# A decode layer on one core: w1 behind the last V, the MLP at the end, and 240 rows of w2 on five DMA engines

## The chip, the cores and the metric

The kernel runs on one core of one Trainium2 chip. The metric is the device time of one execution in microseconds (us), as the median of several runs. One further execution was taken by the hardware profiler; all spans and durations come from it.

## What is computed

One layer for two sequences with one new token each (B = 2, D = 576). The token is normalized, and two branches work on it side by side: attention over the last 4,096 positions of a cache, and a two-layer MLP with a squared ReLU. Everything is bfloat16.

```python
xn = layernorm(x)                                # (2, 576)
q = xn @ wq                                      # 32 heads of 128
k, v = k_cache[:, :, -4096:], v_cache[:, :, -4096:]   # 16 kv heads, 2 q heads each
o = softmax(q k^T * 128**-0.5) v
h = relu(xn @ w1 + b1) ** 2                      # F = 4608
out = x + o @ wo + h @ w2 + b2
```

The weights and the cached keys and values are read once, some 53.6 MB in all; the arithmetic on them is small.

## The kernel before

**Attention in units.** There are 8 units `u` (4 groups of 4 kv heads, times 2 sequences). A unit has one K tile and one V tile of 2 MB (128 partitions of 16 KB). `step(u)` transposes K on TensorE in 8 groups of 8 (`transposes`, L230), copies each group out of PSUM on ScalarE or VectorE (L233, L235), computes scores (L245) and starts the softmax of the unit (L251 to L268), which runs on VectorE, GpSimd and ScalarE. `pv` (L282) multiplies with V two units later. After both sequences of a group, `wo_sel` (a product called `wps`, L301, and a cast `ws`, L304) and `wo_acc` (L209) add the group's part of `o @ wo` to `out_ps`.

**The MLP.** `mlp_h_block(c)` (L322) multiplies the c-th block of 128 rows of `w1` (four blocks, and a folded remainder) with `xn`, one matmul for each 128 of the 4,608 hidden columns: 36 chunks `CH`, each reading its weights with a step of `FR` = 18 columns, so that hidden index `p*18 + r` lies on partition `p`. After the last block VectorE adds b1 and squares (L326, L330) into `hT_sb`. `mlp_o` multiplies each chunk of `hT_sb` with 128 rows of w2, in two halves of 288 columns that go to different partitions of `out_ps` (`out_acc`, L209): two matmuls for a chunk.

**Order and queues.** Nearly all loads are issued on SP's queue in the order written, and each waits on SP until its buffer is free. K, V and the pieces of w2 share a pool `kv` of 6 buffers; wq and w1 share `wbig` of 4. Before, the order is: wq mixed with K of unit 0, K1, w1 blocks 0 and 1, V0, K2, the rest of w1, V1, wo(0), K3; then with each step V(u), wo and K(u+2); at the end the six pieces of w2 (`W2P`, 9 rows a partition down to 1). The h-blocks run inside steps 1 and 2; the outputs of w2 run as its pieces land, mixed with the last unit's `pv` and `wo_acc`. A framework inserts the waits and may shift instructions within an engine's list.

Of the kernel before, what the change touches and what calls it, by code (L numbers as in the profile page):

```python
# [9 lines left out]
BF16 = mybir.dt.bfloat16  # L10
# [6 lines left out]
def kernel(  # L17
# [14 lines left out]
    nc = tc.nc  # L32
    P = 128
    B, Sq, D = A_x.shape
    _, Hkv, Sk, Dh = A_k_cache.shape
    Hq = A_wq.shape[1] // Dh
    F = B_w1.shape[1]
# [11 lines left out]
    NU = NQ * B  # L49
# [9 lines left out]
    LQ = (Hq * Dh) // S  # L59
    L1 = F // S  # L60
    FR = L1 // P
    CH = [(s * L1 + r, FR, P) for s in range(S) for r in range(FR)]
    NFC = len(CH)
    OH = D // 2
    WR = NC * Dh // P
# [44 lines left out]
    def issue_w1(c):  # L110
        issue_w(w1_tiles, B_w1, c, "w1", F, L1)
# [9 lines left out]
    def issue_wo(tq):  # L121
        tl = wopool.tile([P, WR, D], BF16, tag="wo_sb", name=f"wo_{tq}")
        n = NC * Dh
        nc.sync.dma_start(out=tl[:], in_=A_wo[tq * n:(tq + 1) * n, :].rearrange("(p r) n -> p r n", r=WR))
        wo_tiles[tq] = tl

    def issue_w2(s, r0, r1):
        tl = kvpool.tile([P, (r1 - r0) * D], BF16, tag="kv", name=f"w2_{s}_{r0}")
        rows = B_w2[s * L1:(s + 1) * L1, :].rearrange("(p r) n -> p (r n)", r=FR)
        nc.sync.dma_start(out=tl[:], in_=rows[:, r0 * D:r1 * D])  # L130
        w2_tiles[(s, r0)] = tl

    x_sb = const.tile([B, D], BF16, name="x_sb")
    nc.scalar.dma_start(out=x_sb[:], in_=x2d)
# [113 lines left out]
    def softmax(u):  # L248
        sc_ps = sc_tiles.pop(u)
        m1 = work.tile([P, NC], F32, tag="m1", name=f"m1_{u}")  # L250
        nc.vector.tensor_reduce(out=m1[:], in_=sc_ps[:].rearrange("p j c -> p c j"), axis=AX.X, op=ALU.max)  # L251
        m2 = work.tile([P, NC], F32, tag="m2", name=f"m2_{u}")
        nc.vector.tensor_tensor(out=m2[:], in0=m1[:], in1=offm_f, op=ALU.subtract)  # L253
        gmax = work.tile([P, NC], F32, tag="gmax", name=f"gmax_{u}")
        nc.gpsimd.partition_all_reduce(gmax[:], m2[:], channels=P, reduce_op=ReduceOp.max)  # L255
        gm2 = work.tile([P, NC], F32, tag="gm2", name=f"gm2_{u}")
        nc.vector.tensor_tensor(out=gm2[:], in0=gmax[:], in1=offm_f, op=ALU.add)
        sub = work.tile([P, NJ, NC], F32, tag="sub", name=f"sub_{u}")
        nc.vector.tensor_tensor(out=sub[:], in0=sc_ps[:], in1=gm2[:].unsqueeze(1).to_broadcast([P, NJ, NC]),  # L259
                                op=ALU.subtract)  # L260
        pT = keep.tile([P, NJ, NC], BF16, tag="pT", name=f"pT_{u}")
        nc.scalar.activation(out=pT[:], in_=sub[:], func=ACT.Exp, scale=scale)  # L262
        l1 = work.tile([P, NC], F32, tag="l1", name=f"l1_{u}")
        nc.vector.tensor_reduce(out=l1[:], in_=pT[:].rearrange("p j c -> p c j"), axis=AX.X, op=ALU.add)  # L264
        lsum = work.tile([P, NC], F32, tag="lsum", name=f"lsum_{u}")
        nc.gpsimd.partition_all_reduce(lsum[:], l1[:], channels=P, reduce_op=ReduceOp.add)  # L266
        rinv = keep.tile([P, NC], F32, tag="rinv", name=f"rinv_{u}")
        nc.vector.reciprocal(out=rinv[:], in_=lsum[:])  # L268
        pT_tiles[u] = pT
        rinv_tiles[u] = rinv  # L270
# [3 lines left out]
    def pv(u, g):  # L274
        tq, b = divmod(u, B)
        if g == 0:
            oT_cur[u] = psum.tile([P, NC], F32, tag="misc", bufs=2, name=f"oT_ps_{u}")
        oT_ps = oT_cur[u]
        v_sb = v_tiles[u]
        for i in range(JG):  # L280
            j = g * JG + i
            nc.tensor.matmul(oT_ps[:], lhsT=v_sb[:, j * Dh:(j + 1) * Dh], rhs=pT_tiles[u][:, j, :],  # L282
                             start=(j == 0), stop=(j == NJ - 1))
        if g == NG - 1:
            if b == 0:
                oG_tiles[tq] = keep.tile([P, NC, B], BF16, tag="oG", name=f"oG_{tq}")
            nc.vector.tensor_tensor(out=oG_tiles[tq][:, :, b], in0=oT_ps[:], in1=rinv_tiles.pop(u)[:], op=ALU.mult)
            pT_tiles.pop(u)
# [3 lines left out]
    def wo_sel(tq):  # L292
        oG = oG_tiles.pop(tq)
        rr = work.tile([P, WR, NC * B], BF16, tag="rr", name=f"rr_{tq}")
        nc.vector.tensor_tensor(
            out=rr[:],
            in0=oG[:].rearrange("p h b -> p (h b)").unsqueeze(1).to_broadcast([P, WR, NC * B]),
            in1=rmask[:].unsqueeze(2).to_broadcast([P, WR, NC * B]), op=ALU.mult)
        wps = psum.tile([P, WR, B], F32, tag="misc", bufs=2, name=f"wps_{tq}")
        for h in range(NC):  # L300
            nc.tensor.matmul(wps[:], lhsT=sel[:, h, :, :].rearrange("p a c -> p (a c)"),  # L301
                             rhs=rr[:, :, h * B:(h + 1) * B], start=(h == 0), stop=(h == NC - 1))
        ws = work.tile([P, WR, B], BF16, tag="ws", name=f"ws_{tq}")
        nc.vector.tensor_copy(out=ws[:], in_=wps[:])  # L304
        wo_state[tq] = ws
# [9 lines left out]
    def mlp_h_block(c):  # L315
        if c == 0:
            mlp["ps"] = psum.tile([P, NFC, B], F32, tag="misc", bufs=2, name="hT_ps")
            nc.vector.memset(mlp["ps"][:], 0.0)
        hT_ps = mlp["ps"]
        for i, (f0, step, m) in enumerate(CH):  # L320
            lhsT, xc = w_operands(w1_tiles, c, f0, L1, step, m)
            nc.tensor.matmul(hT_ps[0:m, i, :], lhsT=lhsT, rhs=xnT[:, xc, :],  # L322
                             start=(c == 0 and i == 0), stop=(c == KC - 1), skip_group_check=True)
        if c == KC - 1:
            t1 = work.tile([P, NFC, B], F32, tag="t1", name="t1")
            nc.vector.tensor_tensor(out=t1[:], in0=hT_ps[:],  # L326
                                    in1=b1_sb[:].unsqueeze(2).to_broadcast([P, NFC, B]),
                                    op=ALU.add)
            hT_sb = const.tile([P, NFC, B], BF16, name="hT_sb")
            nc.vector.scalar_tensor_tensor(out=hT_sb[:], in0=t1[:], scalar=0.0, in1=t1[:],  # L330
                                           op0=ALU.max, op1=ALU.mult)
            mlp["h"] = hT_sb

    def mlp_o(s, r0, r1, last=False):
        w2_sb = w2_tiles.pop((s, r0))
        for r in range(r0, r1):
            o = (r - r0) * D
            out_acc(mlp["h"][:, s * FR + r, :], lambda a, z: w2_sb[:, o + a:o + z], stop=(last and r == r1 - 1))

    def load_k(u):  # L340
        for f in issue_kv(k_tiles, A_k_cache, u, "k"):
            f()

    def load_v(u):
        for f in issue_kv(v_tiles, A_v_cache, u, "v"):
            f()

    W2P = [(0, 0, 9), (0, 9, 18), (1, 0, 9), (1, 9, 14), (1, 14, 17), (1, 17, 18)]

    load_k(1)  # L350
    issue_w1(0)
    issue_w1(1)
    load_v(0)
    load_k(2)
    for c in range(2, KC):
        issue_w1(c)
    load_v(1)
    issue_wo(0)
    load_k(3)
    def step(u, hooks):  # L360
        for g in range(NG + 2):
            if g < NG:
                transposes(u, g)
            if u >= 2 and 1 <= g <= NG:
                pv(u - 2, g - 1)
            if g >= 2:
                scores(u, g - 2)
            for f in hooks.get(g, ()):
                f()
        softmax(u)  # L370

    def load_next(u):
        load_v(u)
        if u % B == 0:
            issue_wo(u // B)
        if u + 2 < NU:
            load_k(u + 2)

    for g in range(4):
        transposes(0, g)  # L380
    q_block(0)
# [5 lines left out]
    for g in range(NG):  # L387
        scores(0, g)
    softmax(0)
    b1_sb = const.tile([P, NFC], BF16, name="b1_sb")  # L390
    nc.gpsimd.dma_start(out=b1_sb[:].rearrange("p (s r) -> p s r", s=S), in_=B_b1.rearrange("(s p r) -> p s r", s=S, p=P))  # L391
    b2_sb = const.tile([1, D], BF16, name="b2_sb")
    nc.gpsimd.dma_start(out=b2_sb[:], in_=B_b2.rearrange("(o n) -> o n", o=1))
    step(1, {})
    mlp_h_block(0)
    mlp_h_block(1)
    out_acc(ident[:B, :B], lambda a, z: x_sb[:, a:z], start=True)
    out_acc(ones_b[:, :], lambda a, z: b2_sb[:, a:z])
    for u in range(2, NU):
        hooks = {}  # L400
        if u >= 4 and u % B == 0:
            hooks = {3: [lambda t=u // B - 2: wo_sel(t)], 6: [lambda t=u // B - 2: wo_acc(t)]}
        step(u, hooks)
        if u == 2:
            for c in range(2, KC):
                mlp_h_block(c)
        load_next(u)
    for w in W2P:
        issue_w2(*w)
    for g in range(NG):  # L410
        pv(NU - 2, g)
    wo_sel(NQ - 2)
    wo_acc(NQ - 2)
    for g in range(NG):
        pv(NU - 1, g)
    mlp_o(*W2P[0])
    wo_sel(NQ - 1)
    mlp_o(*W2P[1])
    wo_acc(NQ - 1)
    for i in range(2, len(W2P)):  # L420
        mlp_o(*W2P[i], last=(i == len(W2P) - 1))

    fin_sb = work.tile([32 + B, OH], BF16, tag="fin", name="fin_sb")
# [33 lines left out]
```

## Time and profile before

| | |
|---|---|
| median of 3 runs | 137.17 us (137.09 to 137.22) |
| the profiled execution, whole / span | 137.33 / 135.4 us |
| mean granted TensorE clock | 0.761 of full |
| busy: TensorE / VectorE / ScalarE / GpSimd | 76 / 40 / 32 / 7% |
| loaded from HBM | 53.62 MB, 396 GB/s over the span |
| TensorE instructions (matmuls and weight loads) | 2,054 + 2,054 |

How to read the views. The page cuts the span in 40 slices; a digit is a busy share in tenths, PEclk the TensorE clock granted, DMA the mean share of the 16 DMA engines. A line of a group names source line, engine (PE for matmuls, PEld for weight loads), output and inputs, the count, the busy time, and the mean of one in ns; behind the last bar stands the idle time just before them and what ended it. A timeline line gives start, length and count. The chain of waits follows back from the last instruction what released each step. TensorE's ends are modelled, so rates are taken from start to start.

### The profile page before, as it was taken

The page shows a single profiled execution, that of the slowest core. Times are in us where ns is not written, and L with a number is a line of the kernel's source. Part 1 is how long each engine was busy: PE and PEld are TensorE (multiplying, and loading weights), DVE is VectorE, ACT ScalarE, POOL GpSimd, SP SyncE. Part 2 cuts the span into 40 slices and gives each one's busy share as a digit, 9 for nine tenths or more (in the row PEclk, how much of TensorE's full clock was granted, in tenths as well). Part 3 has the DMA queues.
Part 4 walks back from the last instruction along what each step waited for, and adds up shares of the span by engine and source line. Part 5 has one row for each costly group of instructions (what it writes and reads, how often), then busy time and mean ns, then how long its engine had stood idle before and what let it go on. Part 6 is the DMA issues. An engine that isn't in the chain of part 4 may idle for free.

```text
span 135.4 us, 4461 instructions
## 1 busy us (share of the span) xinstructions
PE 102.7 (76%) x2054; PEld 93.3 (69%) x2054; DVE 53.7 (40%) x125; ACT 42.8 (32%) x47; POOL 9.9 (7%) x31
## 2 busy tenths in 40 slices
PE   0049937599978999609992994999599839977791
PEld 0039937589968999609983994899499739554450
DVE  7512411574252433502464345625544564541001
ACT  6704630155013711004601550741155065100000
POOL 7300000110110001100011001100100110110000
PEclk9999995559955995555896589658658999655589
DMA  3999999999999999999999999999999999999940
GB/s 126 401 427 426 426 438 409 415 439 436 411 420 408 439 421 426 415 431 411 436 431 426 421 431 416 406 450 411 436 421 423 425 411 437 416 406 423 393 177 1
DMA packets 5422, 53.90 MB, mean 398 GB/s; under 512 B 646, under 2 KB 796, under 8 KB 1308
## 3 DMA queue, kind: packets, MB, share of 16 engines
q1 hardware_dynamic: 5332, 53.61, 94.4%
q8 instruction: 16, 0.26, 0.8%
q10 hardware_dynamic: 8, 0.00, 0.1%
q0 software_dynamic: 64, 0.01, 0.1%
q14 instruction: 2, 0.02, 0.0%
HBM read 53.62 MB, written 0.00 MB: 396 GB/s over the span
## 4 chain that ended last, share of the span: by engine, by line
DMA 69%; PE 23%; DVE 3%; POOL 2%; issue 1%; ACT 0%; SPq 0%; POOLq 0%
DMA k<-in_A_k_cache_dram 41%; DMA w<-in_B_w_dram 24%; PE kT_ps L230 13%; DMA b_sb<-in_B_b_dram 4%; PE sc_ps L245 3%; PE oT_ps L282 3%; PE out_ps L209 2%; PE qT_ps L218 1%; DVE l L264 1%; POOL b_sb L391 1%; POOL sel L197 1%; DVE sub L259 1%; ACT pT L262 0%; DVE kT L235 0%; DVE fin_sb L424 0%
## 5 line engine op out<-in xcount | busy, mean ns | idle before, releaser
L230 PE MATMUL kT_ps<-ident,k 128*128 128x128 bf16 x512 | 49.7, 267 | 13.9 <-DMA k<-in_A_k_cache_dram 13.6
L230 PEld LDWEIGHTS <-k 128*128 128x128 bf16 x512 | 41.0, 122 | 14.6 <-DMA k<-in_A_k_cache_dram 14.3
L233 ACT COPY kT<-kT_ps 128x1024 bf16<-128x1024 bf16 x32 | 32.2, 1011 | 38.6 <-PE kT_ps L230 38.3
L235 DVE COPY kT<-kT_ps 128x1024 bf16<-128x1024 bf16 x32 | 21.9, 687 | 33.0 <-PE kT_ps L230 33.0
L245 PE MATMUL sc_ps<-qT_all,kT 128*128 128x8 bf16 x512 | 22.1, 168 | 2.8 <-ACT kT L233 1.4
L245 PEld LDWEIGHTS <-kT 128*128 128x128 bf16 x512 | 20.0, 102 | 4.2 <-ACT kT L233 1.8
L282 PE MATMUL oT_ps<-pT,v 128*128 128x8 bf16 x512 | 16.3, 167 | 0.4 <-DMA v<-in_A_v_cache_dram 0.4
L262 ACT ACTIVATE pT<-sub 128x512 bf16<-128x512 f32 x8 | 5.0, 630 | 35.9 <-DVE sub L259 35.9
L282 PEld LDWEIGHTS <-v 128*128 128x128 bf16 x512 | 14.8, 99 | 1.5 <-DMA v<-in_A_v_cache_dram 1.0
L264 DVE TENSOR_REDUCE l<-pT 128x8 f32<-128x512 bf16 x8 | 8.5, 1059 | 4.7 <-ACT pT L262 4.7
L322 PE MATMUL hT_ps<-xnT,w 128*128 128x2 bf16 x144 | 9.8, 201 | 0.0
L322 PEld LDWEIGHTS <-w 128*128 128x128 bf16 x144 | 9.4, 161 | 0.0
L251 DVE TENSOR_REDUCE m<-sc_ps 128x8 f32<-128x512 f32 x8 | 5.5, 692 | 9.1 <-PE sc_ps L245 8.8
L255 POOL PARTITION_ALL_REDUCE gmax<-m x8 | 2.9, 365 | 83.9 <-DVE m L253 77.6
L209 PE MATMUL out_ps<-w,hT_sb 128*2 128x288 bf16 x72 | 7.2, 363 | 1.3 <-DMA w<-in_B_w_dram 1.3
L209 PE MATMUL out_ps<-wo,ws 128*2 128x288 bf16 x64 | 6.8, 359 | 0.3 <-DVE ws L304 0.3
L209 PEld LDWEIGHTS <-hT_sb 128*2 128x2 bf16 x72 | 3.9, 102 | 4.2 <-issue 1.8
L259 DVE TENSOR_TENSOR sub<-sc_ps,gm 128x512 f32<-128x512 f32 x8 | 5.5, 692 | 0.3
L218 PE MATMUL qT_ps<-xnT,wq 128*128 128x2 bf16 x128 | 3.9, 164 | 2.3 <-DMA wq<-in_A_wq_dram 2.0
L218 PEld LDWEIGHTS <-wq 128*128 128x128 bf16 x128 | 3.8, 99 | 2.4 <-DMA wq<-in_A_wq_dram 2.1
L209 PEld LDWEIGHTS <-ws 128*2 128x2 bf16 x64 | 3.1, 99 | 2.8 <-issue 0.6
L266 POOL PARTITION_ALL_REDUCE lsum<-l x8 | 3.2, 398 | 24.5 <-DVE l L264 24.5
(59 smaller groups left out, 35.1 us busy)
## 6 DMA issues: line engine op xcount, KB each, us to landing
v<-in_A_v_cache_dram SPq DMA_DIRECT2D x8, 2048.0 KB, 29.4
k<-in_A_k_cache_dram SPq DMA_DIRECT2D x7, 2048.0 KB, 26.3
w<-in_B_w_dram SPq DMA_DIRECT2D x4, 1152.0 KB, 18.1
wo<-in_A_wo_dram SPq DMA_DIRECT2D x4, 1152.0 KB, 27.5
wq<-in_A_wq_dram SPq DMA_DIRECT2D x4, 1024.0 KB, 9.0
w<-in_B_w_dram SPq DMA_DIRECT2D x3, 1296.0 KB, 22.3
k<-in_A_k_cache_dram SPq DMA_DIRECT2D x2, 1024.0 KB, 8.8
w<-in_B_w_dram SPq DMA_DIRECT2D x1, 720.0 KB, 16.7
```

The lines of the kernel that those rows point to most:

```text
L209: nc.tensor.matmul(out_ps[32 * i:32 * i + B, :], lhsT=lhsT, rhs=rhs_of(i * OH, (i + 1) * OH), start=start, stop=stop, skip_group_check=True)
L218: nc.tensor.matmul(qT_ps[:, h, :], lhsT=lhsT, rhs=xnT[:, xc, :], start=(c == 0 and h == 0), stop=(c == KC - 1), skip_group_check=True)
L230: nc.tensor.transpose(out=kT_ps[:, i * P:(i + 1) * P], in_=k_sb[:, j * Dh:(j + 1) * Dh], identity=ident[:])
L233: nc.scalar.copy(out=kT[:], in_=kT_ps[:])
L235: nc.vector.tensor_copy(out=kT[:], in_=kT_ps[:])
L245: nc.tensor.matmul(sc_ps[:, g * JG + i, :], lhsT=kT[:, i * P:(i + 1) * P], rhs=qT_all[:, b, tq * NC:(tq + 1) * NC], start=True, stop=True)
L251: nc.vector.tensor_reduce(out=m1[:], in_=sc_ps[:].rearrange("p j c -> p c j"), axis=AX.X, op=ALU.max)
L259: nc.vector.tensor_tensor(out=sub[:], in0=sc_ps[:], in1=gm2[:].unsqueeze(1).to_broadcast([P, NJ, NC]), op=ALU.subtract)
L262: nc.scalar.activation(out=pT[:], in_=sub[:], func=ACT.Exp, scale=scale)
L264: nc.vector.tensor_reduce(out=l1[:], in_=pT[:].rearrange("p j c -> p c j"), axis=AX.X, op=ALU.add)
L282: nc.tensor.matmul(oT_ps[:], lhsT=v_sb[:, j * Dh:(j + 1) * Dh], rhs=pT_tiles[u][:, j, :], start=(j == 0), stop=(j == NJ - 1))
L322: nc.tensor.matmul(hT_ps[0:m, i, :], lhsT=lhsT, rhs=xnT[:, xc, :], start=(c == 0 and i == 0), stop=(c == KC - 1), skip_group_check=True)
```

## The change

1. All of w1 is issued later: blocks 0 and 1 right behind V7, then wo(3), the rest of w1, and w2. V and K move up by one unit instead, and wo(1), wo(2), wo(3) get places of their own.
2. The h-blocks move from steps 1 and 2 to the end, around the last `wo_acc`; all outputs of w2 follow them.
3. The second half of w2's rows is cut anew. 16 rows a partition on 128 partitions (`FT`), then 240 rows (`XR` = 12 on each of `XP` = 20 partitions), then 16 rows (`XQ`). The 240 rows load in four transfers whose leading dimension is `XE` = 5, spread among the K and V loads; the 16 rows follow as `w2y_sb`.
4. The chunks change with it: 18 with step 18, 16 with step 16, 12 of 20 hidden columns with step 12, and one of 16; 47 in place of 36. `mlp_x` does the outputs of the last 13 ahead of the others.
5. b1 loads in four pieces behind a memset, and b2 now goes out ahead of them.

```diff
+    XR, XP, XE = 12, 20, 5
+    FT = (L1 - XR * XP) // P
+    CH = [(r, FR, P) for r in range(FR)] + [(L1 + r, FT, P) for r in range(FT)]
+    CH += [(FX0 + r, XR, XP) for r in range(XR)] + [(FX0 + XR * XP, 1, XQ)]
...
+    def issue_w2x():
+        if x_parts:
+            i = x_parts.pop(0)
+            rows = B_w2[FX0:FX0 + XR * XP, :].rearrange("(e i r) n -> i e (r n)", e=XE, r=XR)
+            nc.sync.dma_start(out=w2x_sb[i:XP:XP // XE, :], in_=rows[i])
+            if not x_parts:
+                nc.sync.dma_start(out=w2y_sb[:], in_=B_w2[FX0 + XR * XP:F, :])
...
+    def mlp_x():
+        for i, (f0, step, m) in enumerate(CH[FR + FT:]):
+            w = w2x_sb[0:m, i * D:(i + 1) * D] if m == XP else w2y_sb[:]
+            out_acc(mlp["h"][0:m, FR + FT + i, :], lambda a, z: w[:, a:z])
...
-    W2P = [(0, 0, 9), (0, 9, 18), (1, 0, 9), (1, 9, 14), (1, 14, 17), (1, 17, 18)]
+    W2P = [(0, 0, 9), (0, 9, 18), (1, 0, 9), (1, 9, 13), (1, 13, 15), (1, 15, 16)]
...
     load_k(1)
-    issue_w1(0)
-    issue_w1(1)
     load_v(0)
     load_k(2)
-    for c in range(2, KC):
-        issue_w1(c)
     load_v(1)
...
-    mlp_h_block(0)
-    mlp_h_block(1)
+    load_k(4)
+    issue_wo(1)
...
+        if u + 1 < NU - 1:
+            load_v(u + 1)
+        if u + 3 < NU:
+            load_k(u + 3)
+        if u == 4:
+            issue_wo(2)
+        if u == 5:
+            load_v(NU - 1)
+            issue_w1(0)
+            issue_w1(1)
+        if u == 6:
+            issue_wo(3)
             for c in range(2, KC):
-                mlp_h_block(c)
-        load_next(u)
-    for w in W2P:
+                issue_w1(c)
+            for w in W2P[:2]:
+                issue_w2(*w)
+    for w in W2P[2:4]:
         issue_w2(*w)
     for g in range(NG):
         pv(NU - 2, g)
+    issue_w2(*W2P[4])
     wo_sel(NQ - 2)
     wo_acc(NQ - 2)
     for g in range(NG):
         pv(NU - 1, g)
-    mlp_o(*W2P[0])
+    issue_w2(*W2P[5])
+    mlp_h_block(0)
+    mlp_h_block(1)
     wo_sel(NQ - 1)
-    mlp_o(*W2P[1])
     wo_acc(NQ - 1)
-    for i in range(2, len(W2P)):
+    for c in range(2, KC):
+        mlp_h_block(c)
+    mlp_x()
+    for i in range(len(W2P)):
         mlp_o(*W2P[i], last=(i == len(W2P) - 1))
```

## The prediction

> **What bounds the kernel now.** I read the page's slices first, then the chain of waits, then windows over the last microseconds, then the timeline of TensorE and the groups by line.
>
> ```profile
> PE   0049937599978999609992994999599839977791
> PEclk9999995559955995555896589658658999655589
> DMA  3999999999999999999999999999999999999940
> q1 hardware_dynamic: 5332, 53.61, 94.4%
> q8 instruction: 16, 0.26, 0.8%
> ```
>
> The DMA row is 9 from the second slice to the last but two: the transfers bound this kernel, 53.62 MB in 132 us. TensorE is only partly busy, and its granted clock swings between half and full. The chain of waits ends on the transfers:
>
> ```profile
> 116.33 15.67 DMA w<-in_B_w_dram
> 132.00 0.04 issue
> 132.04 0.67 PE out_ps L209 x8
> 132.72 0.03 issue
> 132.74 0.45 DVE fin_sb L424
> ```
>
> The last pieces of w2 land at 132.0, eight matmuls follow, then the copy and the store: 2.7 us from the last matmul's end (132.7) to the span's end. But the transfers do not end together (columns: window, length, PE, PEld, DVE, ACT, POOL busy, clock, DMA share, GB/s):
>
> ```profile
> 127.00:128.00 1.00, 1.00 (x12) 0.57 (x10) 0.00 (x0) 0.00 (x0) 0.00 (x0) 0.50 1.05 423
> 128.00:129.00 1.00, 1.00 (x12) 0.55 (x10) 0.00 (x0) 0.00 (x0) 0.00 (x0) 0.50 0.80 310
> 129.00:130.00 1.00, 1.00 (x12) 0.53 (x8) 0.00 (x0) 0.00 (x0) 0.00 (x0) 0.52 0.67 255
> 130.00:131.00 1.00, 1.00 (x22) 0.71 (x18) 0.00 (x0) 0.00 (x0) 0.00 (x0) 1.00 0.42 165
> 131.00:131.90 0.90, 0.89 (x16) 0.51 (x11) 0.00 (x0) 0.00 (x0) 0.00 (x0) 1.00 0.30 106
> ```
>
> From 128 on the DMA share sinks: about six of the sixteen engines are done near 129, seven work on until 132. So the end is set by late engines, and a perfect levelling would give 0.2+0.33+0.58+0.63 = 1.7 us.
>
> [...]
>
> **The change, part by part.** *Transfers.* The bytes are the same. 240 of w2's rows (0.276 MB) leave the even share: eleven engines carry 17.3 KB less, 0.65 us at 26.6 GB/s per engine (425 over 16); the five carry 38 KB more, 1.43 us. If the five are among the early engines, the last landing moves from 132.4 to 131.7; if among the late, to 133.8. The profile does not name engines; I take the former, and keep -0.65 and +1.4. The loads that wait for buffers stay far ahead: in the new SP order k5 waits for step 2's transposes (near 42 us) and is due at 71; w2's last piece waits for pv(7) (near 109) and is due at 131. Five more issues on SP cost 0.3 to 0.5 us each beside that lead: nothing. On POOL a memset and three more small b1 loads (some 1 us each, as L391) delay `sel` (busy from 4.75 now) to about 6; first need is after 55 us: nothing. b2 is now issued ahead of b1 and lands up to 1 us sooner, which TensorE only turns into a longer wait for wq (2.05 us idle at 19.5): nothing.
>
> *The middle.* Five h-blocks leave steps 1 and 2: 5 x 2.24 us. TensorE has idle time there, so no gain, and it waits longer for k.
>
> *The end.* This is the price. Counting bytes back from 131.7 at 0.418 MB/us (k1 landing at 25.7, k2 at 41.1, k3 at 60.9 fit that line), k7 lands at 91.5, v7 at 104.3, w1 pieces at 107, 109.9, 115.6, 118.4, 119.8, with wo(3) at 112.7, and w2 from 123 to 131.7. TensorE's built order after the scores of unit 7 is pv(6), wps(2), wo(2), pv(7), wps(3), h(0), h(1), wo(3), h(2), h(3), h(rem), then 26 matmuls on the five-engine rows and 68 on the rest.
>
> ```profile
> 50.13 2.37 PE L322 MATMUL hT_ps<-xnT,w 128*128 128x2 bf16 x36
> 52.37 2.37 PE L322 MATMUL hT_ps<-xnT,w_rem 128*128 128x2 bf16 x36
> 119.73 1.87 PE L282 MATMUL oT_ps<-pT,v 128*128 128x8 bf16 x64 [0.44 <-DMA v<-in_A_v_cache_dram]
> 126.02 2.32 PE L209 MATMUL out_ps<-w,hT_sb 128*2 128x288 bf16 x18 [0.82 <-DMA w<-in_B_w_dram]
> 128.13 2.04 PE L209 MATMUL out_ps<-wo,ws 128*2 128x288 bf16 x16
> 130.01 1.88 PE L209 MATMUL out_ps<-w,hT_sb 128*2 128x288 bf16 x28
> L218 PEld LDWEIGHTS <-wq 128*128 128x128 bf16 x128 | 3.8, 99 | 2.4 <-DMA wq<-in_A_wq_dram 2.1
> ```
>
> An h-block of 36 takes 2.24 us start to start, 62 ns each, at either clock. The q-block on contiguous weights takes 32 in 0.99 us, 31 each. h reads w1's columns with a step of 18, so the weight load sets its pace. [...] One block: 2.1 + 0.4 = 2.5 us. An output pair costs 0.235 us at half clock (16 matmuls in 1.88 us from 128.13), about 0.12 at full (14 pairs in 1.6).
>
> Step 7 starts at 91.5 and takes 7.5 to 8.7 without pv (24 transposes in 2.74 us at half clock; before, 8.8 with 1.1 of pv inside). Scores end near 99.6. The cast of ws(2) stands behind softmax(7) in VectorE's order: 5.0 us from the row maximum to the reciprocal (115.71 to 120.6), 0.4 more. wo(2) waits for it on TensorE and pv(7) is queued behind: 105.1. Then wo(2) 2.0, pv(7) 1.8, its scaling, spreading and wps(3) 0.95: 109.9. h(0), h(1): 114.9. wo(3) 2.0: 116.9. h(2), h(3), h(rem) at 2.5, all after their landings: 124.4. Two VectorE operations of 0.23 each at 72 columns, 0.25 at 94, with handovers 0.75: hT is ready at 125.1. [...] Last matmul: 125.1 + 8.2 + 0.3 latency = 133.6, against 132.7. Sum: +0.9; I take 0.2 off, because step 7 runs at full clock in a third of such cases or so (7.5 instead of the 8.1 used): +0.7. The profiled execution took 137.33 us, span 135.4 plus 1.9 around it; the median of three is 137.17. From the median: **137.9 us, slower**.
>
> **Rivals.** *The output work hides (not slower).* Place: TensorE from 116 on. If hT is ready by 123.5, 1.6 us earlier than worked out, the last output matmuls wait for the last landing again, and the levelling comes through whole: -0.65, 136.5 us. It needs h-blocks of 2.0 us or less (full-column loads under 50 ns), or the full clock at the start of the outputs (47 x 0.12 = 5.6 us, in time even from 125.7). For it: the DMA-bound tail is short, 0.67 us. Against it: 144 loads at a median of 162 ns with the step of 18, 96 without. It decides from 124.2 for break-even.
> *Short loads are not short.* All 47 at 62 ns make 2.9 us a block; three blocks behind landed data and two before add 2.1: +2.8, 140.0 us. For it: no row of the profile shows a strided load of few columns.
> *The five engines are the late ones.* Last landing 133.8, then 0.7: +1.4, 138.6 us. For it: about ten of sixteen engines still work past 129, and the profile does not say which. [...] One in five.
> *The change not made as said*: the built SP order has all w1 pieces behind v7, and 5-row transfers among the k and v loads; dismissed.
>
> **How the numbers follow.** Forecast 0.45 (own range 137.2 to 138.8), hidden 0.18, all loads long 0.17, late five 0.20. Measurement tells about 0.2%, 0.27 us, from no change. Faster takes nearly all of the first rival and the very lowest end of the forecast: 0.18. Within 0.2%: 0.12, the forecast's low end. Slower: 0.70. The range runs from 136.5 to 140.3, which takes in both bounds of the levelling and the long loads, and leaves out a step of 16 at 75 ns with a late clock, and h at 31 ns with a clock already full.
>
> **What would show it.** Right: no DMA wait above 0.5 us before the last output group; PEclk 0.50 when the outputs start near 125; DMA share falling to 0 about 1.5 us before the last matmul; the chain ending in out_ps and hT_ps matmuls instead of w2. The levelling is right if the sinking of the DMA share after 128 becomes a steeper one ending 0.65 us sooner. Wrong: the last output group still ended by a DMA wait, blocks of 47 far from 2.5 us, or a share near 0.3 (five engines) in the last microseconds.

## The result, and the profile after

The changed kernel takes 142.88 us (median of 4 runs, 141.15 to 144.69) against 137.19 us: a ratio of 1.033, 95% interval 1.0258 to 1.0402. Run again unchanged beside the first experiments it took 143.74 us (143.15 to 145.03), ratio 1.0466 (1.042 to 1.0512). It is slower, as forecast, but by 5.7 to 6.3 us where 0.7 was forecast and 140.3 was the top of the range. Medians here are over all runs of a kernel; ratios are to the kernel before on the same chip and leave out runs more than 1.5% above the fastest of that kernel (two of the four here, 13 of 20 in e6, three of four in e4, which has no ratio), among them the first profiled run and those of e4, e6, e13 and e15. The lines below are from the second set's profiled execution (143.76 us, span 141.7).

The slices of the page:

```profile
PE   0089637797779979809999797959972899998991
PEclk9999975579655555955995999985685555555589
DMA  4999999999999999999999999999999999997000
```

Before, the DMA row went on until the last slice but one. Now three slices at the end are empty of transfers, and TensorE works through two of them and into the third. The end of the chain of waits (start, length, what):

```profile
103.15 0.64 PE sc_ps L264 x16
...
108.88 2.08 PE out_ps L228 x13
110.96 1.81 PE oT_ps L301 x64
113.71 5.36 PE hT_ps L341 x92
119.12 1.94 PE out_ps L228 x15
121.07 8.30 PE hT_ps L341 x141
129.99 8.81 PE out_ps L228 x81
138.83 0.45 DVE fin_sb L464
```

No transfer is in it. The chain runs through the last unit's softmax, wo(2), the h-blocks and the outputs, as worked out, but it starts late and its last two links are long. Windows (window, length, busy PE, PEld, DVE, ACT, POOL, clock, DMA share, GB/s):

```profile
129.00:130.00 1.00, 0.36 (x12) 0.27 (x11) 0.51 (x2) 0.00 (x0) 0.00 (x0) 0.50 0.84 322
130.00:131.00 1.00, 1.00 (x10) 0.53 (x12) 0.00 (x0) 0.00 (x0) 0.00 (x0) 0.50 0.58 218
131.00:132.00 1.00, 1.00 (x12) 0.52 (x10) 0.00 (x0) 0.00 (x0) 0.00 (x0) 0.50 0.01 2
132.00:135.50 3.50, 3.50 (x32) 1.63 (x28) 0.00 (x0) 0.00 (x0) 0.00 (x0) 0.50 0.00 0
136.00:138.00 2.00, 2.00 (x36) 1.39 (x34) 0.00 (x0) 0.00 (x0) 0.00 (x0) 1.00 0.00 0
```

The transfers were levelled: the share falls from 0.58 to 0.01 at 131, and the last landing (the moment when a transfer's end is signalled) is at 131.53, where it was 132.37. In the first profile's trace 16 packets are in flight most of the time, and each of the four row transfers is five packets of 13,824 bytes; those of the first two transfers overlap, some 0.52 us each, which fits five engines. No view names an engine. But TensorE needs 7.3 us more, and until about 135.8 it has only half its clock (0.50).

### The profile page after: what moved, and what is told of

Its sections match the earlier page's. It is cut to its first block, busy times and chain, and to the rows that moved or that the text cites. A ratio compares the mean times of both kernels' runs of the same rounds, so it can differ in the third digit from the quotient of the medians.

```text
span 141.4 us, 4625 instructions
## 1 busy us (share of the span) xinstructions
PE 107.4 (76%) x2131; PEld 94.8 (67%) x2131; DVE 53.0 (37%) x125; ACT 42.1 (30%) x47; POOL 11.4 (8%) x35
## 4 chain that ended last, share of the span: by engine, by line
PE 49%; DVE 20%; DMA 12%; ACT 6%; issue 4%; POOL 4%; SPq 2%; POOLq 0%; ACTq 0%
PE kT_ps L249 13%; DMA wq_rem<-in_A_wq_dram 12%; PE out_ps L228 11%; PE hT_ps L341 10%; PE sc_ps L264 9%; DVE l L283 6%; PE oT_ps L301 6%; DVE sub L278 4%; ACT pT L281 4%; DVE m L270 2%; DVE kT L254 2%; ACT kT L252 2%; POOL gmax L274 2%; POOL lsum L285 2%; SPq L107 1%
## 5 line engine op out<-in xcount | busy, mean ns | idle before, releaser
L249 PE MATMUL kT_ps<-ident,k 128*128 128x128 bf16 x512 | 47.3, 259 | 2.8 <-DMA k<-in_A_k_cache_dram 1.7
L249 PEld LDWEIGHTS <-k 128*128 128x128 bf16 x512 | 39.0, 118 | 3.2 <-DMA k<-in_A_k_cache_dram 1.9
L254 DVE COPY kT<-kT_ps 128x1024 bf16<-128x1024 bf16 x32 | 21.4, 682 | 22.0 <-PE kT_ps L249 22.0
L264 PEld LDWEIGHTS <-kT 128*128 128x128 bf16 x512 | 19.0, 101 | 11.2 <-ACT kT L252 5.7
L228 PE MATMUL out_ps<-wo,ws 128*2 128x288 bf16 x64 | 7.5, 400 | 5.8 <-DVE ws L323 5.8
L341 PEld LDWEIGHTS <-w 128*128 128x128 bf16 (+2 forms) x188 | 10.9, 154 | 0.6 <-issue 0.5
L341 PE MATMUL hT_ps<-xnT,w 128*128 128x2 bf16 (+2 forms) x188 | 11.2, 194 | 0.0
L228 PEld LDWEIGHTS <-ws 128*2 128x2 bf16 x64 | 3.8, 106 | 7.7 <-DVE ws L323 6.0
L228 PEld LDWEIGHTS <-hT_sb 128*2 128x2 bf16 (+2 forms) x94 | 5.0, 106 | 4.8 <-DVE hT_sb L349 0.7
L228 PE MATMUL out_ps<-w,hT_sb 128*2 128x288 bf16 x68 | 6.2, 359 | 0.0
```

What stands on the lines that cost most here:

```text
L228: nc.tensor.matmul(out_ps[32 * i:32 * i + B, :], lhsT=lhsT, rhs=rhs_of(i * OH, (i + 1) * OH), start=start, stop=stop, skip_group_check=True)
L249: nc.tensor.transpose(out=kT_ps[:, i * P:(i + 1) * P], in_=k_sb[:, j * Dh:(j + 1) * Dh], identity=ident[:])
L254: nc.vector.tensor_copy(out=kT[:], in_=kT_ps[:])
L264: nc.tensor.matmul(sc_ps[:, g * JG + i, :], lhsT=kT[:, i * P:(i + 1) * P], rhs=qT_all[:, b, tq * NC:(tq + 1) * NC], start=True, stop=True)
```

## The experiments

All lines named "L..." are those of the kernel shown; kernels with edits shift by a few.

### One part of the change at a time

**e1_cut_only: the old order of loads, with the new cut.** The five-engine rows load in the changed kernel's way and their outputs follow step 4.

```diff
 # kernel before, CH, issue_w2, issue_w2x, b1 and W2P as in the changed kernel
         step(u, hooks)
...
+        if u == 4:
+            mlp_x()
```

> The kernel before with only part 3 to 5 of the change: w2 is cut anew, 240 of its rows load on five engines, 47 chunks, and their 13 outputs run behind step 4; w1, K, V keep their old places. Theory 'TensorE's tail': the loss comes from the moved MLP alone, and the levelling is real (last landing in the changed kernel 131.5 against 132.4): 0.6 to 0.9 us faster than before, 136.3 to 136.6. Rival 'the five engines or the 47 chunks cost': as slow as before or slower, 137.2 or more, with the DMA share sinking from 128 on as before.

137.67 us, ratio 1.0014 (0.9989 to 1.0038): no difference, and a miss. The end of its chain:

```profile
105.13 21.50 DMA w<-in_B_w_dram
126.63 0.04 issue
126.67 6.18 PE out_ps L228 x56
132.85 0.02 issue
132.87 0.45 DVE fin_sb L458
```

From 126.67 on TensorE waits for nothing, at half clock until 130.7. The last landing, 132.21, is also only 0.16 us sooner than before, so this execution had little of the levelling to use. The kernel before could not have used much of it either. There TensorE ran from 126.02 to 131.89 unbroken, and ahead of its last eight matmuls it waited only 0.16 us:

```profile
132.04 0.65 PE L209 MATMUL out_ps<-w,hT_sb 128*2 128x288 bf16 x8 [0.16 <-DMA w<-in_B_w_dram]
```

So its tail had two bounds, the transfers and TensorE, with almost nothing between them.

**e2_move_only: the move, with the old cut.**

```diff
-    CH = [(r, FR, P) for r in range(FR)] + [(L1 + r, FT, P) for r in range(FT)]
-    CH += [(FX0 + r, XR, XP) for r in range(XR)] + [(FX0 + XR * XP, 1, XQ)]
+    CH = [(s * L1 + r, FR, P) for s in range(S) for r in range(FR)]
...
-    mlp_x()
```

> The changed kernel with w2 cut as before (36 chunks, no five-engine transfers). Theory 'TensorE's tail': still bound by TensorE at the end, but with 11 output pairs fewer (11 x 0.12 to 0.24 = 1.3 to 2.6 us) and h-blocks 0.4 us shorter each (2.0): 3.3 to 4.6 us below the changed kernel's 141.7, so 137.1 to 138.4; the last landing goes back to about 132.4. Rival 'the recut is what costs': back to 137.2 or below, with the chain ending on w2.

137.36 us, ratio 1.0002 (0.9985 to 1.0018): the move alone is free. Its timeline of TensorE (start, length, what; in brackets the wait ahead of it):

```profile
104.54 2.08 PE L227 MATMUL out_ps<-wo,ws 128*2 128x288 bf16 x16 [2.94 <-DVE ws L322]
...
123.73 2.32 PE L227 MATMUL out_ps<-w,hT_sb 128*2 128x288 bf16 x18 [0.59 <-DVE hT_sb L348]
126.27 2.32 PE L227 MATMUL out_ps<-w,hT_sb 128*2 128x288 bf16 x18 [0.22 <-DMA w<-in_B_w_dram]
129.37 3.85 PE L227 MATMUL out_ps<-w,hT_sb 128*2 128x288 bf16 x36 [0.77 <-DMA w<-in_B_w_dram]
```

This is the forecast's chain: scores(7) end at 99.4 (99.6 forecast), wo(2) at 104.5 (105.1), hT at 123.7 with the shorter blocks. So neither part costs anything measurable alone; together they cost 6 us. What the recut does inside the moved tail was the question.

### The parts of the tail, each taken out of the changed kernel

**e5_after_again** is the changed kernel itself, for comparison with the three that follow.

> The changed kernel itself, once more, for a profile of a further execution and for the scatter of its times. [...] Rival 'transfers differ from run to run': the last landing moves with the time.

Its last landing was 131.53, where the first profile (143.47 us) had 131.54. Only these two executions were profiled, so whether the transfers have a part in the scatter from 141.15 to 145.03 is not shown.

**e6_no_x_out** leaves out the 26 output matmuls on the five-engine rows and the 16 rows behind them (`mlp_x()` removed), so the part of the result that these 256 hidden units give is missing.

> The changed kernel without the 26 output matmuls on the five-engine rows and the 16 rows behind them; it leaves out the part of the result that 256 hidden units give, all else is done. Theory: 13 pairs at 0.12 to 0.24 us stand between hT and the rest: 1.6 to 3.1 us less, 138.6 to 140.1. Rival 'hidden by the wait for w2': no change.

139.73 us (137.16 to 141.64), 4.0 less than the changed kernel's 143.74; ratio to before 1.0028 (0.9997 to 1.0059), from its seven shortest runs. Thirteen pairs for 256 rows cost about what they take in the changed kernel's timeline, 3.2 us from 129.99 to 133.20, and some more.

**e7_no_x_h** leaves out the 65 short matmuls of the h-blocks, so h is not computed for the rows that they feed.

```diff
-        for i, (f0, step, m) in enumerate(CH):
+        for i, (f0, step, m) in enumerate(CH[:FR + FT]):
```

> The changed kernel with its 13 short chunks left out of the five h-blocks (65 matmuls of at most 20 columns); 256 hidden units stay zero before the bias, all else is done. Theory: a block shrinks from 2.75 to 2.15 us; all five stand on the chain: 3.0 us less, 138.7. Rival 'a short chunk is short' (30 ns): 65 x 0.03 = 2.0 less, 139.7.

141.64 us, ratio 1.0258 (1.0202 to 1.0315): 2.1 less than 143.74. Sixty-eight full chunks follow one another in 4.29 us (111.21 to 115.50), 63 ns each. The changed kernel's 94 from 121.00 to 126.52 make 2.76 us a block of 47; less 34 at 63 ns that leaves 0.62 us for 13 short ones, some 48 ns each. From wo(2) to the first outputs e7's profile is 3.0 us shorter than the changed kernel's, as expected, but in it the clock turned full only 8.8 us after the outputs began, and the outputs took 10.2 us where the changed kernel's took 8.8. The changed kernel's groups by shape fit the slow short loads (busy time and mean ns of one behind the bar):

```profile
L341 PEld LDWEIGHTS <-w 128*128 128x128 bf16 x136 | 8.7, 165 | 0.5 <-issue 0.5
L341 PEld LDWEIGHTS <-w 128*20 128x20 bf16 x48 | 2.1, 124 | 0.1
```

One load of a sixth of the columns takes three quarters of the time (loads overlap, so these times are longer than the pace).

**e4_h_contig** reads adjacent columns in all h matmuls, so h is computed for hidden units in an order that does not fit the rows of w2.

```diff
-    CH = [(r, FR, P) for r in range(FR)] + [(L1 + r, FT, P) for r in range(FT)]
-    CH += [(FX0 + r, XR, XP) for r in range(XR)] + [(FX0 + XR * XP, 1, XQ)]
+    CH = [(r * P, 1, P) for r in range(FR)] + [(L1 + r * P, 1, P) for r in range(FT)]
+    CH += [(FX0 + r * XP, 1, XP) for r in range(XR)] + [(FX0 + XR * XP, 1, XQ)]
```

> The changed kernel with each h chunk reading neighbouring columns of w1 (step 1) in place of step 18, 16 or 12. It leaves out the matching order of hidden units, so rows of w2 meet other units; the amount of work is the same. Theory 'the step sets the pace of the weight load': 27 to 31 ns each, a block 1.3 to 1.5 us in place of 2.7 to 2.8; five blocks save 6 to 7 us, of which the end takes what is left above the last landing: 137 to 138 at most, perhaps bound by the last h-block's data. Rival 'small matmuls have a floor near 60 ns': no change.

The median is 139.89 us (137.12 to 140.92), above what was expected; only the shortest of four runs is in the expected range. The step theory holds: 92 matmuls in 2.65 us start to start, 29 ns each. But part of it is lost again just behind:

```profile
114.67 2.81 PE L341 MATMUL hT_ps<-xnT,w 128*128 128x2 bf16 x92
...
124.53 0.78 PE L341 MATMUL hT_ps<-xnT,w_rem 128*128 128x2 bf16 x22 [1.26 <-issue]
125.95 3.04 PE L228 MATMUL out_ps<-w2x_sb,hT_sb 20*2 20x288 bf16 x24 [0.64 <-DVE hT_sb L349]
```

The 1.26 us of "issue" is time in which TensorE waited for nothing that the profile shows.

### Why the chain starts late

In the changed kernel wo(0) stands on TensorE for ws(0), and K of the next unit is transposed late:

```profile
59.21 0.74 PE L301 MATMUL oT_ps<-pT,v 128*128 128x8 bf16 x24
63.58 2.08 PE L228 MATMUL out_ps<-wo,ws 128*2 128x288 bf16 x16 [3.62 <-DVE ws L323]
...
66.04 2.20 PE L249 MATMUL kT_ps<-ident,k 128*128 128x128 bf16 x24
```

"Move only" does not have this wait. The two programs differ on TensorE in one place ahead of the h-blocks: in step 3, "move only" has pv and the product wps(0) between the scores, and on VectorE the cast ws(0) ahead of softmax(3). The changed kernel has all scores of step 3 first, and ws(0) behind that softmax. The framework built this from the same calls; apart from the loads of b1 and the parts that TensorE meets only later (h-blocks and outputs), only the row loads differ.

**e3_ws_early** takes the casts out of softmax's way.

```diff
-    def wo_sel(tq):
+    def wo_sel(tq, act=False):
...
+        if act:
+            nc.scalar.copy(out=ws[:], in_=wps[:])
+        else:
+            nc.vector.tensor_copy(out=ws[:], in_=wps[:])
...
-            hooks = {3: [lambda t=u // B - 2: wo_sel(t)], 6: [lambda t=u // B - 2: wo_acc(t)]}
+            hooks = {3: [lambda t=u // B - 2: wo_sel(t, act=True)], 6: [lambda t=u // B - 2: wo_acc(t)]}
+        if u == NU - 1:
+            hooks = {NG + 1: [lambda: wo_sel(NQ - 2)]}
...
-    wo_sel(NQ - 2)
```

> The changed kernel with the casts ws of groups 0 and 1 on ScalarE and wo_sel(2) written ahead of softmax(7), so that no output matmul of wo waits behind a softmax on VectorE. Theory 'a chain of TensorE and VectorE from 48 us on': the two waits (5.8 us) shorten the chain by most of their length, 3 to 5 us: 137 to 139. Rival 'only the end counts' (the wait at 59 is absorbed by later waits for K): at most 3 us. Rival 'transfers': no change from 141.7.

139.0 us, ratio 1.0121 (1.0057 to 1.0185): 4.7 less than 143.74. This takes away most of the wait at wo(0) (0.71 us is left, for wo itself) and the wait for ws(2), together.

**e9_rows_once: the five row transfers together behind V2.** That alone gives the built order of "move only".

```diff
     load_v(2)
+    for _ in range(5):
+        issue_w2x()
...
-        if u >= 3:
-            issue_w2x()
...
-        if u >= 1:
-            issue_w2x()
```

> The changed kernel with one edit: the four five-engine row loads (and the last 16 rows) are issued together behind V2, where the changed kernel spreads them behind V1, K3, V2 and K4. With that the built order of TensorE up to the h-blocks is the one of 'move only': wps(0) stands ahead of the last scores of step 3, and ws(0) ahead of softmax(3) on VectorE. Theory (the built order put ws(0) behind softmax(3), and TensorE stood 2.6 to 3.6 us at wo(0) and never made it up): no wait at wo(0), scores(7) end at 99.4 to 100.2 as in 'move only', hT near 125.8 (its 123.7 plus five short-chunk surcharges of 0.4), 94 outputs in 9.0 to 9.4, last matmul about 135.0, 139.0 to 139.8 in all. Rival (the order is an accident that costs nothing; the recut itself makes it late): 142 to 144 as the changed kernel.

141.16 us (139.92 to 142.6), ratio 1.0224 (1.0156 to 1.0292): 2.6 less than the changed kernel, 1.4 above the expected range. The places are right:

```profile
59.35 1.15 PE L228 MATMUL out_ps<-wo,ws 128*2 128x288 bf16 x16
...
91.89 2.74 PE L249 MATMUL kT_ps<-ident,k 128*128 128x128 bf16 x24 [1.88 <-DMA k<-in_A_k_cache_dram]
...
125.47 3.04 PE L228 MATMUL out_ps<-w2x_sb,hT_sb 20*2 20x288 bf16 x24 [0.64 <-DVE hT_sb L349]
```

No wait at wo(0), TensorE waits for K7 again, scores(7) end at 99.3, hT is ready at 125.47 where 125.8 was expected. The last matmul ends at 134.94. The profiled execution of this kernel was its shortest run, 139.92. Below, e13 and e14 differ in the same edit alone, and their medians don't differ (140.96 and 140.86), though e13's runs reach 146.4.

**e10_move_flip: the other direction.** "Move only" with the row transfers put back, unread, gets the changed kernel's order.

```diff
-    x_parts = []
+    x_parts = list(range(XP // XE))
```

> 'Move only' (36 whole chunks) with the five-engine row loads put back as transfers alone, in the changed kernel's places; nothing reads them, and the rows they carry load a second time in the ordinary pieces. TensorE's built order up to the h-blocks becomes the changed kernel's (wps(0) and PV behind all scores of step 3). Theory (order): TensorE waits about 3 us for ws(0) near 60, scores(7) end 101.5 to 103.5, hT 126 to 127.5, 90 outputs at half clock in 8.6 to 9.0, last matmul 135 to 136.5, 139.3 to 141 in all. Rival (order costs nothing, only 276 KB more are moved): 137.3 to 138.2.

138.16 us, ratio 1.0053 (1.0025 to 1.0081): only 0.8 over "move only", and within the rival's range, in which the order costs nothing and only 276 KB more are moved. In the profile K7 lands 0.69 us later than in "move only" (92.56 against 91.87), so the bytes account for most of the 0.8. The wait at wo(0) is there (2.35 us, wo(0) at 61.19), but TensorE still comes to K7 early and waits 1.31 us for it. **The order costs slack, and only what exceeds the slack costs time.** In the changed kernel wo(0) came 2.4 us later than in this one; the clock was 0.54 on average from 50 to 58 us there, and 0.91 here. TensorE reached K7 at 93.70 with no wait left; then came 1.48 us of "issue", and most of step 7 at half clock. In the first profile of the changed kernel wo(0) came only 0.75 us later than here, at 61.94, and TensorE still reached K7 at 93.86 with no wait left. In e7, which is the changed kernel up to its h-blocks, wo(0) began at 61.43, and a little slack was left at K7 (e7 first, then the changed kernel):

```profile
91.85 0.45 PE L249 MATMUL kT_ps<-ident,k 128*128 128x128 bf16 x5 [0.32 <-DMA k<-in_A_k_cache_dram]
93.30 2.19 PE L249 MATMUL kT_ps<-ident,k 128*128 128x128 bf16 x19 [1.00 <-issue]
...
93.70 0.44 PE L249 MATMUL kT_ps<-ident,k 128*128 128x128 bf16 x5
95.61 2.19 PE L249 MATMUL kT_ps<-ident,k 128*128 128x128 bf16 x19 [1.48 <-issue]
```

So with the same order wo(2) can begin 2.35 us apart (106.53 and 108.88). Over all profiles with the recut, it began at 106.5 to 110.0 in the six with this order and wo_sel(2) in its old place (the changed kernel twice, e4, e6, e7, e13), and at 104.4 and 106.2 in the two with the order repaired (e9, e14).

**e11_rows_once_sel and e12_move_sel: wo_sel(2) ahead of softmax(7)**, on e9 and on e2.

```diff
+        if u == NU - 1:
+            hooks = {NG + 1: [lambda: wo_sel(NQ - 2)]}
         step(u, hooks)
...
-    wo_sel(NQ - 2)
     wo_acc(NQ - 2)
```

> The kernel with the rows loaded together behind V2, and wo_sel(2) ahead of softmax(7) as well, so that ws(2) does not stand behind that softmax on VectorE. If the wait of 2.9 us at wo(2) is on the path: hT near 123, outputs of 94 matmuls in 9.0, last matmul 132.0 to 132.6 against a last landing of 131.5: 136.3 to 137.1, that is 2.2 to 3 us under the kernel without this edit, and at or just under the kernel before. If the path is elsewhere: as without the edit, 139 to 139.8.

> 'Move only' (36 whole chunks, no five-engine rows) with wo_sel(2) ahead of softmax(7). The last landing of 132.4 to 132.5 and what follows it set the end there: 137.0 to 137.4, no different from 'move only' although TensorE is ready 2 us earlier. If TensorE's half-speed outputs set the end instead: 136.3 to 136.9.

With the recut 139.45 us, ratio 1.0116 (1.0069 to 1.0163), 1.7 less than without the edit but 2.3 over what was expected. V7 lands late enough to take back much of the wait (1.27 us ahead of pv(7)), w1 takes another 0.71 us ahead of the third h-block, and the outputs start at 124.80, not 123. Without the recut 137.49, ratio 1.0001 (0.9974 to 1.0028), no difference, as expected: there w2's landing sets the end. A wait of 2.6 to 2.9 us at the same instruction is worth 1.7 us in one kernel's median and nothing in the other's.

### The clock in the outputs

**e8_cut_warm** puts eight transposes of a landed w2 piece, work for the clock alone, ahead of the second piece's outputs in e1.

```diff
     wo_sel(NQ - 1)
+    dense(w20, 8)     # 8 transposes of the first w2 piece, read by nothing
     mlp_o(*W2P[1])
```

> e1 (the cut alone, w1 early) with 8 more transposes of a landed w2 piece, into a PSUM tile that nothing reads, between the outputs of the first and the second w2 piece, where TensorE waits 0.8 us for the second. [...] Rival 'the tail is bound by the landings plus handovers': 137.3 as e1.

137.5 us, ratio 1.0006 (0.9977 to 1.0036): no gain that can be measured. The clock did turn sooner: it was full from about 127.2 instead of 130.7, the last matmul at 132.2, and TensorE waits for w2 again. Its last landing is at 131.89. What it frees, up to e1's landing, is 0.6 us of e1's span at most.

In the changed kernel and in e3, e4, e7, e9 and e11 the matmuls on 20 rows come first, and the clock turned full 5.8 to 8.8 us after outputs began, which is 2.6 to 5.6 us after those on 128 rows began. Where 128-row outputs come first (before, e1, e2, e6, e10, e12) it was 2.8 to 4.7 us after the last wait among the outputs (in e10, 4.7 us of them ahead of a wait of 0.76 us had not turned it). So perhaps 20-row matmuls do not raise the clock, a guess for the next three runs.

**e13_after_x_mid, e14_rows_once_x_mid, e15_sel_x_mid** place them behind the second piece, in the changed kernel, in e9 and in e11.

```diff
-    mlp_x()
     for i in range(len(W2P)):
+        if i == 2:
+            mlp_x()
         mlp_o(*W2P[i], last=(i == len(W2P) - 1))
```

> The changed kernel with one edit: the 26 output matmuls on the five-engine rows come behind the second w2 piece instead of first; same matmuls, same transfers, same built order up to hT. Theory (matmuls on 20 rows don't count as work for the clock, so that it turns full 2.3 to 5 us after the first 128-row outputs and not after the first outputs): hT ready at 129 to 130 as before, full clock 3 to 4.7 us after that instead of 5.8 to 7, 94 outputs in 7.0 to 7.6 instead of 9.0 to 9.4, 1.8 to 2.4 us under the changed kernel (141 to 142 where that stands at 143.3). Rival (the clock turns a given time after outputs begin, whatever their rows): 9.0 to 9.4 and no gain.

> The rows loaded together behind V2 (so the built order of 'move only'), and the same edit: five-engine outputs behind the second w2 piece. Both theories stacked: hT near 125.5, outputs in 7.0 to 7.5, last matmul 132.5 to 133.1 where it was 134.9: 2 us under the kernel without the edit, 138.0 to 139.2. If the 20-row matmuls have nothing to do with the clock: 140 to 142 as without it.

> As the last, and wo_sel(2) ahead of softmax(7): hT near 124.8, outputs in 7.0 to 7.5, last matmul 131.9 to 132.4, no more than 0.9 behind the last landing of 131.5: 136.8 to 137.4, level with the kernel before. Without an effect of the 20 rows on the clock: 139 to 139.7.

Medians 140.96 (139.35 to 146.4), 140.86 and 138.4 us (137.02 to 142.4); ratios 1.0168 (1.0112 to 1.0225), 1.0213 (1.0167 to 1.0259) and 1.0035 (1.0005 to 1.0065). Against the kernels that they were made from: some 2.8 less, nothing, and 1.0 less; e14 is where its rival had it, that the 20-row matmuls have nothing to do with the clock. The profile of e13 is of its longest run, 146.4 us:

```profile
129.79 4.48 PE L228 MATMUL out_ps<-w,hT_sb 128*2 128x288 bf16 x36 [0.64 <-DVE hT_sb L349]
134.20 3.04 PE L228 MATMUL out_ps<-w2x_sb,hT_sb 20*2 20x288 bf16 x24
...
137.41 4.00 PE L228 MATMUL out_ps<-w,hT_sb 128*2 128x288 bf16 x32
```

TensorE is busy throughout for 11.6 us, 94 matmuls at half clock to the last; e15's profile, also of its longest run, has the same 11.6 us. In e14 the clock turned 5.2 us after the start. In the middle, the 20-row work cuts the 128-row work into 4.4 and 4.0 us.

**e17_sel_x_late** puts them behind the third piece (`i == 3`).

> Rows loaded together behind V2, wo_sel(2) ahead of softmax(7), and the five-engine outputs behind the third w2 piece, so that 54 matmuls on 128 rows come first without a gap of 20-row work. If full clock needs 2.5 to 5.3 us of 128-row outputs (what the runs with five-engine outputs first or second left), it comes 2.5 to 5.3 us after hT at 124.2 to 125, that is before 130.3, in every run; the last piece then ends at 131.7 to 132.6: 136.8 to 137.6, and with less scatter than with the rows behind the second piece (137.0 to 142.4), where 4.4 us of 128-row work were sometimes too short. If 20-row matmuls count like others, place makes no difference: a median of 138.4 and runs up to 142 again.

138.49 us, ratio 1.0077 (1.0053 to 1.0102). The scatter shrank as expected, 138.07 to 139.74 against 137.02 to 142.4; the median did not. In the profile:

```profile
125.77 6.24 PE L228 MATMUL out_ps<-w,hT_sb 128*2 128x288 bf16 x54 [0.64 <-DVE hT_sb L349]
131.94 1.63 PE L228 MATMUL out_ps<-w2x_sb,hT_sb 20*2 20x288 bf16 x24
```

The clock turned 5.7 us after the start, just past the 5.3 that was expected as the most, and hT came 0.8 us late. Once full, it stayed full through the 20-row matmuls, 24 in 1.47 us.

**e16_sel_x_mid40 and e18_sel_x_late40: the same 240 rows on 40 partitions**, `XR, XP = 6, 40`, eight transfers; on e15 all behind V2, on e17 four behind V2 and four behind wo(2).

> As the last, but the 240 rows lie on 40 partitions with 6 rows each (eight transfers to five engines each instead of four): 6 short chunks instead of 12. Five h-blocks lose 6 short loads each of some 45 ns, 1.35 us in all, and 12 output matmuls go: hT near 123.4 to 123.9, the last landing of 131.5 sets the end and TensorE waits for w2 again, last matmul 131.7 to 132.0: 136.3 to 136.8, 0.5 to 0.9 under the kernel before. [...]

> As the last, with the 240 rows on 40 partitions of 6 rows each (6 short chunks instead of 12), their eight transfers four at a time behind V2 and behind wo(2), because eight at once behind V2 let the queue run dry for 4 us. If that was the only fault: five h-blocks are 30 short loads of some 45 ns lighter, hT at 123 to 123.8, last matmul 131.7 to 132.2: 136.3 to 137.1, at or under the kernel before. If transfers are held up again: over 139.

143.06 us (1.0399, 1.0359 to 1.044) and 140.66 us (1.0228, 1.0207 to 1.0249). Both fail, for two reasons. The transfers of e16 stand still for 4 us, as the page's row of GB/s (one figure a slice) and then SP's waits (total, times, longest) show:

```profile
GB/s 131 420 405 419 417 438 438 428 419 419 418 425 427 433 291 37 386 400 452 419 428 442 442 396 424 442 403 442 419 405 424 422 413 419 423 432 427 387 102 1
```

```profile
SPq L148 <- DMA v<-in_A_v_cache_dram: 13.0, 3, 4.6
SPq L148 <- DMA k<-in_A_k_cache_dram: 12.5, 3, 4.3
```

L148 issues the row transfers. They write to a tile of their own, and yet SP waits there for V and K to land: the small transfers wait for earlier ones to finish, and the next 2 MB load behind them is issued too late. Why they have to wait is not shown. In e18 the row has 280 in one slice. And a block of 41 takes 2.78 us start to start, no less than one of 47: halving the number of short chunks saved nothing, since 2.78 us less 34 full ones at 63 ns leaves some 90 ns for each of the seven. Why is open.

## Why the prediction was wrong

**Right: the direction and the mechanism.** TensorE's tail took over from the transfers, no DMA wait stood ahead of the last outputs, the clock was half (0.50) when they began, and the DMA share fell to 0 well ahead of the last matmul. The levelling was right in size: the last landing moved by 0.83 us (0.65 forecast), to 131.53, and the rival of the late five, which put it at 133.8, falls. That the same five engines carry all four transfers, and that the other eleven carry less for it, was the author's estimate: no run shows it, only the five packets a transfer and the landing. Why some transfers end late was not tested. "All 47 loads at 62 ns" falls too (some 48 ns for the short ones, midway between 62 and the forecast's 0.4 us for 13, some 31 each), and so does the rival that hides the output work.

**Wrong: the sum.** Last matmul 133.6 forecast; 138.5 and 138.8 in the two profiled executions. Three terms failed.

1. *"Step 7 starts at 91.5 … Scores end near 99.6."* They ended at 102.9 and 103.8. The step took K7's landing for the start, as though TensorE would be waiting for it, and 8.1 us for its length. K7 landed in time (91.9 in e9), but TensorE came to it at 93.9 and 93.7, and in the second profile the step then took 10.1 us, 1.48 of them "issue" and most of it at half clock. I compared the built order only from unit 7's scores on; the change of order was in step 3. The later waits follow: wo(2) began at 108.0 and 108.9 where 105.1 was forecast, with its wait for ws(2) of 3.3 us as foreseen. This is 3.8 of the 5.2 us of the second profile. With the order repaired (e9) the profile's last matmul is at 134.94, 3.85 earlier, but that was e9's shortest run: the medians differ by 2.6, and those of e13 and e14 by nothing. So the order took the slack, clock and "issue" waits decide from there how much is lost, and the share of each is not settled.
2. *"One block: 2.1 + 0.4 = 2.5 us."* It took 2.7 to 2.8: 5.43 us for the first two and 8.35 for the other three. The 0.4, some 31 ns for each of the 13 short chunks, was the author's estimate, and no run shows it: they took some 48 ns each (e5 and e7), and five blocks come to 1.3 us more. Nor does a run show the 75 ns that the range names for a step of 16: the 68 full chunks of e7, with steps of 18 and 16, took 63 ns each.
3. *"125.1 + 8.2 + 0.3 latency = 133.6"*. The 8.2 us for the 47 output pairs was the author's estimate of when the clock would rise, and no run shows it. They took 8.8 and 9.4 us, where 8.5 was in the sum with its latency: 0.3 to 0.9 more, the rest of the miss. In the kernel before, the clock went from 0.50 to 1.00 at 130.0, 4.0 us after the outputs at 126.02, and in its h-blocks it had fallen to 0.50 at 37.8 and 51.4; in the changed kernel it was 0.50 through the last h-blocks and rose 5.8 and 7.0 us after the first output. In the 17 profiles with a turn that nothing was added to bring about, the clock turned 2.6 to 5.7 us after unbroken 128-row outputs began; what sets the time within these bounds is not shown. The 26 matmuls on 20 or 16 rows, 3.2 us at half clock, came ahead of those in the changed kernel. That matmuls on few rows do less to raise the clock, no run proves: the kernels with the 20 rows first fit, and so do the longest runs of e13 and e15; in e14 the turn fell 0.8 us into the 20-row stretch, and e17's neither helps nor contradicts.

**The reading of before was incomplete.** "The transfers bound this kernel" came from a full DMA row and a chain that ended in a landing. But TensorE waited only 0.16 us ahead of its last eight matmuls, so an earlier landing had next to nothing to give at that clock. The cut alone earned nothing that can be measured (e1, e8), though there the last landing moved by only 0.16 and 0.48 us. A tail of 0.67 us behind the landing told what one bound costs, not how far off the other was.

**No version beat the kernel before.** The best complete one with both parts of the change is e15, ratio 1.0035; those with one part (e1, e2, e8, e12) are level with before. The count points to the reason: 256 rows in 13 short chunks need 13 output pairs and 65 h matmuls where two full chunks need 2 pairs and 10, on an engine that had no time to give, to save 0.8 us of landing.

## What to carry to other kernels

Work placed on few partitions to balance transfers can cost a compute engine nearly as much as work on all of them (here an output matmul at half clock took some 118 ns on 20 rows and 118 to 122 on 128, and a short h matmul 48 ns against 63): count its instructions on the engine at the tail before counting the bytes saved. When a change adds transfers among the loads, compare the built order of every engine over the whole program, and look for a cast or copy that has moved behind a long reduction. A wait costs only what exceeds the slack ahead of the next landing (e10: a wait of 2.35 us at wo(0), 0.8 us in the time); price it in the kernel where it stands.

## What was not expected of the hardware

- A weight load of 20 strided columns took 124 ns on average against 165 for 128 columns (e5); h matmuls followed one another at some 48 and 63 ns (e5, e7). With adjacent columns it was 29 ns (e4).
- Blocks of 41 with 6 short chunks of 40 columns took as long as blocks of 47 with 12 of 20 columns: 2.78 and 2.76 us.
- In the longest runs of e13 and e15, 11.6 us of unbroken matmuls, 3.2 of them on 20 or 16 rows in the middle, did not raise the clock; in the 17 other profiles without added work it turned 2.6 to 5.7 us after unbroken 128-row outputs began.
- With nine small transfers in a row (e16), SP waited at them, up to 4.6 us at a time, until earlier 2 MB loads had landed, and the transfers fell to 37 GB/s for one slice of 3.5 us.
